# Gated linear attention and a normed MLP: the order of chunk 0, the rounding of the weights, and attention two chunks ahead

## The chip, the cores and the metric

One Trainium2 chip, one core of it. The metric is the device time of one execution in microseconds (us); the time before is 559.5 us, the median of three runs (559.44 to 559.54). The engines are named as in the profile: PE (TensorE, matrix products), DVE (VectorE), ACT (ScalarE), POOL (GpSimd) and SP (SyncE, which here only issues DMAs).

## The reference

Two blocks, one after the other. The first is a gated linear recurrence over 4 batches, 8 heads, 768 positions and heads of 48:

```
state = alpha[:, :, t, :, None] * state + k[:, :, t] (outer) v[:, :, t]
y[:, :, t] = q[:, :, t] @ state
```

Its output, reordered to (4, 768, 384), is `x` of the second block:

```
xn  = (x - mean) / sqrt(var + 1e-06) * g_ln
out = x + relu(xn @ w_ch1) @ w_ch2
```

`w_ch1` is 384 x 1536 and `w_ch2` 1536 x 384. Both arrive as 64-bit floats; everything else is 32-bit.

## The kernel before

**Chunks.** The 768 positions are cut into 6 chunks of 128 (`NCB`). Within a chunk the recurrence is done as matrix products, for each of the 4 batches apart, in five steps: `decays` (logarithm of alpha, running sum by a triangular matmul into `lps`, the exponentials `ek` and `eq`, `k*ek` on POOL and `q*eq` on DVE, the row of chunk gates sent through DRAM, the loads of the next chunk), `turn` (transposes into `tps`, copied to `qkT`), `scores` (`aps`, copied under a mask into `at`), `attend` (`yps`, the new state through `sps`, the copy to `x`, its mean and variance, the normed `xn`), and `turn_x` (transposes of `xn` into `xps`, multiplied by g into `xT`). `attention_steps(c)` lists these 20 steps as a wave: batch b is one step behind batch b - 1.

**The MLP.** For a chunk, all four batches together, `hidden(c, j)` makes one of the 12 blocks of 128 hidden units (3 contraction steps into `hps`, then a relu into `hT` on ACT for even j, on DVE for odd j). `project(c, b, js)` makes a third of the second product of one batch (`ops`), and with the last third adds `x` into `ob` and sends it out. In the profile a 32-bit product appears as two matmul instructions.

**Rounding.** The weights are loaded as 64-bit words in 12 pieces (6 of w1, then 6 of w2), each into one of three staging buffers (`STAGED`), and turned into 32-bit floats by seven DVE instructions a piece (`round_weights`, L129 to L138). `take_weights(i)` rounds piece i and then issues the load of piece i + 3 into the buffer that came free.

**Order.** `run(main, side)` lists the steps of `main` with those of `side` spread evenly between them. That list is the text's order; the framework's planner then orders each engine's instructions by priority of the text and by when its model has them ready, so that neighbours in the text may be mixed. Each engine works through its own list in order, and so does the queue of SP, in which a DMA that waits for a buffer holds up those behind it. Before the change the list is: attention of chunk 0 with w1's six roundings spread over it; the first product of chunk 0 with w2's six roundings and the first six steps of chunk 1's attention; then the second product of chunk 0 with the rest of them; and from then on, for each chunk, both products with the attention of the next chunk.

```
run(attention_steps(0), rounds[:half])
for c in range(NCB):
    side = attention_steps(c + 1) if c + 1 < NCB else []
    mlp = mlp_steps(c)
    if c == 0:
        run(mlp[:NJ], [go for i in range(half) for go in (rounds[half + i], side[i])])
        run(mlp[NJ:], side[half:])
    else:
        run(mlp, side)
```

PSUM has eight banks, shared out by tag: three for `lps`, `tps` and `aps`, two for `yps`, `sps` and `xps`, two for `hps`, one for `ops`.

Of the kernel before, what the change touches and what calls it, by code (L numbers as in the profile page):

```python
# [9 lines left out]
FP32 = mybir.dt.float32  # L10
# [4 lines left out]
AOP = mybir.AluOpType  # L15
# [6 lines left out]
def kernel(  # L22
# [8 lines left out]
    w_ch2: bass.AP,  # L31
    out: bass.AP,
):

# [14 lines left out]
    nc = tc.nc  # L51

    B, S, H, D = q.shape
    DM = H * D
    DF = w_ch1.shape[1]
    P = 128
    NCB = S // P
    NP = H // 2
    R = 64 + D
    NF = DM // P  # L60
    NJ = DF // P
# [3 lines left out]
    cpool = ctx.enter_context(tc.tile_pool(name="const", bufs=1))  # L65
    raw = ctx.enter_context(tc.tile_pool(name="raw", bufs=B))
    stage = ctx.enter_context(tc.tile_pool(name="stage", bufs=STAGED))
    work = ctx.enter_context(tc.tile_pool(name="work", bufs=2))
# [34 lines left out]
    pieces = []  # L103
    for i in range(NJ // 2):
        cs, js = slice(2 * i * P, 2 * (i + 1) * P), slice(2 * i, 2 * (i + 1))
        pieces.append((w1[:, :, cs], w1_src[:, :, cs]))
        pieces.append((w2[:, js], w2_src[:, js]))
    pieces = pieces[::2] + pieces[1::2]
    staged = {}

    def load_weights(i):
        if i >= len(pieces):
            return
        dst, src = pieces[i]
        if src.dtype != FP32:
            dst = staged[i] = stage.tile(list(dst.shape), INT64, name="ws", tag="ws")
        nc.sync.dma_start(dst, src)

    def round_weights(i):

        dst = pieces[i][0]
        ws = staged.pop(i)
        words = ws.bitcast(INT32).rearrange("p a (c t) -> p a c t", t=2)
        lo, hi = words[:, :, :, 0], words[:, :, :, 1]
        ts, stt = nc.vector.tensor_scalar, nc.vector.scalar_tensor_tensor
        ts(out=dst.bitcast(INT32), in0=hi, scalar1=0x000FFFFF, scalar2=0x00100000,  # L129
           op0=AOP.bitwise_and, op1=AOP.bitwise_or)  # L130
        stt(out=dst, in0=lo.bitcast(UINT32), scalar=2.0 ** -32, in1=dst.bitcast(INT32),  # L131
            op0=AOP.mult, op1=AOP.add)
        ts(out=lo, in0=hi, scalar1=0x7FF00000, scalar2=None, op0=AOP.bitwise_and)
        ts(out=lo, in0=lo, scalar1=float(896 << 20), scalar2=0.0,
           op0=AOP.subtract, op1=AOP.max)
        ts(out=hi, in0=hi, scalar1=-(1 << 31), scalar2=None, op0=AOP.bitwise_and)
        stt(out=hi, in0=lo, scalar=8.0, in1=hi, op0=AOP.mult, op1=AOP.add)  # L137
        stt(out=dst, in0=dst, scalar=2.0 ** -20, in1=hi.bitcast(FP32),  # L138
            op0=AOP.mult, op1=AOP.mult)

    def take_weights(i):
        if i in staged:
            round_weights(i)
        load_weights(i + STAGED)

    for i in range(STAGED):
# [1 line left out]

    eps = cpool.tile([P, 1], FP32, name="eps")
    nc.vector.memset(eps, EPS)  # L150


    eqs = [cpool.tile([P, NP, 2, 64], FP32, name=f"eq{b}") for b in range(B)]
# [38 lines left out]
    def turn(c, b):  # L192
        qkT = work.tile([R, 2, NP, P], FP32, name="qkT", tag="qkT", bufs=3)
        for i in range(2):
            tps = ps.tile([R, NP, P], FP32, name="tps", tag="a", bufs=3)
            for p in range(NP):
                nc.tensor.transpose(  # L197
                    tps[:, p], qks[b][:, i, p].rearrange("p a b -> p (a b)")[:, :R], ident)
            if i == 0:
                nc.scalar.copy(out=qkT[:, i], in_=tps)  # L200
            else:
                nc.vector.tensor_copy(out=qkT[:, i], in_=tps)  # L202
        qkT_of[c, b] = qkT
# [15 lines left out]
    def attend(c, b):  # L219
# [13 lines left out]
        if c + 1 < NCB:  # L233
# [6 lines left out]
            for i, s in heads:  # L240
# [1 line left out]
            st = sts[b].rearrange("p a b d -> p a (b d)")  # L242
            nc.gpsimd.tensor_mul(  # L243
                st, st, gate_of.pop((c, b)).unsqueeze(2).broadcast_to([P, NP, 2 * D]))
        x = work.tile([P, DM], FP32, name="x", tag="x", bufs=2 * B)
        nc.scalar.copy(out=x, in_=yps.rearrange("p a b d -> p (a b d)"))  # L246
        stats = work.tile([P, 6], FP32, name="stats", tag="stats")
        mv = work.tile([P, 2], FP32, name="mv", tag="mv")
# [10 lines left out]
    def turn_x(c, b):  # L259
        if b == 0:  # L260
            xT_of[c] = work.tile([P, NF, B, P], FP32, name="xT", tag="xT")
        xn = xn_of.pop((c, b))
        xps = ps.tile([P, NF, P], FP32, name="xps", tag="s")
        for f in range(NF):
            nc.tensor.transpose(xps[:, f], xn[:, f * P:(f + 1) * P], ident)  # L265
        nc.vector.tensor_mul(xT_of[c][:, :, b], xps,  # L266
                             g_col.unsqueeze(2).broadcast_to([P, NF, P]))

    def hidden(c, j):
        if j == 0:
            hT_of[c] = work.tile([P, NJ, B, P], FP32, name="hT", tag="hT", bufs=1)
        hps = ps.tile([P, B, P], FP32, name="hps", tag="h")
        for f in range(NF):
            nc.tensor.matmul(hps, w1[:, f, j * P:(j + 1) * P], xT_of[c][:, f],  # L276
                             start=(f == 0), stop=(f == NF - 1))
        if j % 2 == 0:
            nc.scalar.activation(out=hT_of[c][:, j], in_=hps, func=AFT.Relu)  # L279
        else:  # L280
            nc.vector.tensor_scalar_max(hT_of[c][:, j], in0=hps, scalar1=0.0)  # L281

    ops_of = {}

    def project(c, b, js):
        if js[0] == 0:
            ops_of[b] = ps.tile([P, DM], FP32, name="ops", tag="o", bufs=1)
        for j in js:
            nc.tensor.matmul(ops_of[b], hT_of[c][:, j, b], w2[:, j],  # L289
                             start=(j == 0), stop=(j == NJ - 1))  # L290
        if js[-1] == NJ - 1:
            ob = work.tile([P, DM], FP32, name="ob", tag="ob", bufs=3)
            nc.vector.tensor_add(ob, ops_of.pop(b), x_of.pop((c, b)))  # L293
            nc.sync.dma_start(out[b, c * P:(c + 1) * P], ob)

    def attention_steps(c):

        stages = [decays, turn, scores, attend, turn_x]
        return [lambda f=stages[w - b], b=b: f(c, b)
                for w in range(B + len(stages) - 1)  # L300
                for b in range(B) if 0 <= w - b < len(stages)]

    def mlp_steps(c):
        thirds = [range(i * NJ // 3, (i + 1) * NJ // 3) for i in range(3)]
        return ([lambda j=j: hidden(c, j) for j in range(NJ)]
                + [lambda b=b, js=js: project(c, b, js) for b in range(B) for js in thirds])

    def run(main, side):

        done = 0  # L310
        for i, step in enumerate(main):
            step()
            due = (i + 1) * len(side) // len(main)
            for go in side[done:due]:
                go()
            done = due

    half = len(pieces) // 2
    rounds = [lambda i=i: take_weights(i) for i in range(len(pieces))]
    run(attention_steps(0), rounds[:half])  # L320
    for c in range(NCB):
        side = attention_steps(c + 1) if c + 1 < NCB else []
        mlp = mlp_steps(c)
        if c == 0:
            run(mlp[:NJ], [go for i in range(half) for go in (rounds[half + i], side[i])])
            run(mlp[NJ:], side[half:])
        else:
            run(mlp, side)


# [27 lines left out]
```

## Time and profile before

| | before |
|---|---|
| median of three runs | 559.5 us |
| the profiled execution's own time | 557.12 us |
| its span | 555.3 us |
| PE busy | 519.0 us (93%) |
| DVE busy | 225.0 us (41%) |
| ACT busy | 90.1 us (16%) |
| POOL busy | 50.4 us (9%) |
| granted clock of PE, mean | 0.966 |
| share of PE in the chain that ended last | 88%, of DVE 7%, of DMA 3% |

The table is from the page of the profiled execution. Busy time is what an engine spent on instructions; matmuls are pipelined, so their busy times overlap and a PE that is busy all the time is not one at its peak. The clock is the share of TensorE's full speed that was granted.

### The profile page before, as it was taken

The page shows a single profiled execution, that of the slowest core. Times are in us where ns is not written, and L with a number is a line of the kernel's source. Part 1 is how long each engine was busy: PE and PEld are TensorE (multiplying, and loading weights), DVE is VectorE, ACT ScalarE, POOL GpSimd, SP SyncE. Part 2 cuts the span into 40 slices and gives each one's busy share as a digit, 9 for nine tenths or more (in the row PEclk, how much of TensorE's full clock was granted, in tenths as well). Part 3 has the DMA queues.
Part 4 walks back from the last instruction along what each step waited for, and adds up shares of the span by engine and source line. Part 5 has one row for each costly group of instructions (what it writes and reads, how often), then busy time and mean ns, then how long its engine had stood idle before and what let it go on. Part 6 is the DMA issues. An engine that isn't in the chain of part 4 may idle for free.

```text
span 555.3 us, 7418 instructions
## 1 busy us (share of the span) xinstructions
PE 519.0 (93%) x3112; PEld 303.0 (55%) x3112; DVE 225.0 (41%) x385; ACT 90.1 (16%) x205; POOL 50.4 (9%) x54
## 2 busy tenths in 40 slices
PE   4665699999899999999999999999999999999997
PEld 2454244666545566645566644666645566644553
DVE  2999999533422432423432423331433322311000
ACT  3211021111212210122200032200122110101000
POOL 3232000110200100100100010010101000000000
PEclk9856699999999999999999999999999999999999
DMA  8975343220121110122120011110000000000000
GB/s 271 301 215 191 96 146 99 59 86 30 56 60 44 43 43 30 44 54 63 28 71 30 30 57 45 29 43 15 15 15 0 1 14 15 16 14 1 4 24 28
DMA packets 32489, 33.72 MB, mean 61 GB/s; under 512 B 13108, under 2 KB 28596, under 8 KB 32456
## 3 DMA queue, kind: packets, MB, share of 16 engines
q1 hardware_dynamic: 31912, 33.12, 19.5%
q8 instruction: 24, 0.39, 0.3%
q10 hardware_dynamic: 544, 0.13, 0.1%
q14 instruction: 9, 0.07, 0.0%
HBM read 28.49 MB, written 4.76 MB: 60 GB/s over the span
## 4 chain that ended last, share of the span: by engine, by line
PE 88%; DVE 7%; DMA 3%; issue 1%; POOL 0%; SPq 0%; POOLq 0%; DVEq 0%
PE ops L289 35%; PE hps L276 34%; PE aps L212 4%; PE yps L231 4%; PE yps L226 3%; PE tps L197 3%; PE lps L176 2%; PE sps L238 1%; PE xps L265 1%; DMA ws<-in_moe_w_ch_dram 1%; DVE ws L137 1%; DVE w L131 1%; DVE w L129 1%; DVE w L138 1%; DMA ra<-in_alpha_dram 1%
## 5 line engine op out<-in xcount | busy, mean ns | idle before, releaser
L289 PE MATMUL ops<-w,hT 128*128 128x384 f32 x576 | 198.3, 492 | 2.0 <-DVE ob L293 2.0
L276 PE MATMUL hps<-xT,w 128*128 128x512 f32 x432 | 195.8, 601 | 1.8 <-DVE xT L266 1.8
L289 PEld LDWEIGHTS ops<-w,hT 128*128 128x128 f32 x576 | 105.5, 190 | 69.7 <-DVE ob L293 3.8
L276 PEld LDWEIGHTS hps<-xT,w 128*128 128x128 f32 x432 | 80.3, 192 | 93.4 <-issue 84.8
L281 DVE TENSOR_SCALAR hT<-hps 128x512 f32<-128x512 f32 x36 | 24.8, 690 | 83.7 <-PE hps L276 83.4
L181 POOL TENSOR_TENSOR qk<-rk,ek 128x384 f32<-128x384 f32 x24 | 28.5, 1187 | 212.6 <-ACT ek L179 205.2
L279 ACT ACTIVATE hT<-hps 128x512 f32<-128x512 f32 x36 | 21.5, 597 | 117.9 <-PE hps L276 117.9
L215 DVE COPY_PREDICATED at<-consts,aps 128x512 f32<-128x512 int32 x48 | 32.5, 719 | 18.9 <-PE aps L212 18.8
L231 PE MATMUL yps<-rv,at 128*64 128x48 f32 x768 | 39.8, 230 | 0.0
L231 PEld LDWEIGHTS yps<-rv,at 128*64 128x64 f32 x768 | 35.5, 149 | 3.9 <-issue 3.9
L241 DVE TENSOR_TENSOR st<-sps,st 64x192 f32<-64x192 f32 (+1 forms) x40 | 14.2, 355 | 57.0 <-PE sps L238 56.7
L293 DVE TENSOR_TENSOR ob<-ops,x 128x384 f32<-128x384 f32 x24 | 13.4, 558 | 55.8 <-PE ops L289 55.4
L246 ACT COPY x<-yps 128x384 f32<-128x384 f32 x24 | 11.5, 478 | 150.4 <-PE yps L231 150.3
L243 POOL TENSOR_TENSOR st<-st,gate 128x384 f32<-128x384 f32 x20 | 18.6, 928 | 182.4 <-DVE st L241 151.4
L197 PE MATMUL tps<-consts,qk 128*112 128x128 f32 x192 | 27.8, 286 | 7.2 <-DVE qk L182 5.4
L197 PEld LDWEIGHTS tps<-consts,qk 128*112 128x112 f32 x192 | 22.9, 139 | 19.4 <-issue 9.7
L182 DVE TENSOR_TENSOR qk<-rq,eq 128x384 f32<-128x384 f32 x24 | 23.3, 969 | 25.1 <-ACT eq L180 25.1
L212 PEld LDWEIGHTS aps<-qkT 48*128 48x128 f32 x384 | 25.7, 204 | 13.7 <-issue 9.0
L212 PE MATMUL aps<-qkT 48*128 48x128 f32 x384 | 30.7, 303 | 0.0
L176 PE MATMUL lps<-la,consts 128*128 128x384 f32 x48 | 22.1, 544 | 8.2 <-ACT la L174 4.3
L226 PE MATMUL yps<-st,qkT 112*64 112x96 f32 x320 | 29.7, 259 | 0.0
L202 DVE COPY qkT<-tps 112x512 f32<-112x512 f32 x24 | 16.5, 689 | 31.3 <-PE tps L197 31.3
(33 smaller groups left out, 252.9 us busy)
## 6 DMA issues: line engine op xcount, KB each, us to landing
ws<-in_moe_w_ch_dram SPq DMA_DIRECT2D x12, 768.0 KB, 4.7
ra<-in_alpha_dram SPq DMA_DIRECT2D x24, 192.0 KB, 3.0
rk<-in_k_dram SPq DMA_DIRECT2D x24, 192.0 KB, 3.4
rq<-in_q_dram SPq DMA_DIRECT2D x24, 192.0 KB, 2.5
rv<-in_v_dram SPq DMA_DIRECT2D x24, 192.0 KB, 2.4
out_dram<-ob SPq DMA_DIRECT2D x24, 192.0 KB, 1.8
row<-eq SPq DMA_DIRECT2D x20, 2.0 KB
gate<-row SPq DMA_DIRECT2D x20, 2.0 KB, 2.9
```

The lines of the kernel that those rows point to most:

```text
L176: nc.tensor.matmul(lps[:, :DM], tri, la, start=True, stop=True)
L181: nc.gpsimd.tensor_mul(qk[:, 1, :, :D], raws.pop(("k", c, b)), ek)
L182: nc.vector.tensor_mul(qk[:, 0, :, :D], raws.pop(("q", c, b)), eq)
L197: nc.tensor.transpose(tps[:, p], qks[b][:, i, p].rearrange("p a b -> p (a b)")[:, :R], ident)
L212: nc.tensor.matmul(aps[i][:, p], qkT[rows, 1, p], qkT[rows, 0, p], start=True, stop=True)
L215: nc.vector.copy_predicated(out=at[:, i], data=aps[i], mask=mask.unsqueeze(1).broadcast_to([P, NP, P]))
L226: nc.tensor.matmul(yps[s, p].rearrange("p a b -> p (a b)"), qkT[:, 0, p, s], sts[b][:R, p].rearrange("p a b -> p (a b)"), start=True, stop ...
L231: nc.tensor.matmul(yps[s, p, i], at[:, i, p, s], vt[:, 2 * p + i], start=(c == 0), stop=(c == 0 or i == 1))
L276: nc.tensor.matmul(hps, w1[:, f, j * P:(j + 1) * P], xT_of[c][:, f], start=(f == 0), stop=(f == NF - 1))
L279: nc.scalar.activation(out=hT_of[c][:, j], in_=hps, func=AFT.Relu)
L281: nc.vector.tensor_scalar_max(hT_of[c][:, j], in0=hps, scalar1=0.0)
L289: nc.tensor.matmul(ops_of[b], hT_of[c][:, j, b], w2[:, j], start=(j == 0), stop=(j == NJ - 1))
```

## The change

The attention of chunk 0 is listed alone. Then come w1's roundings, each followed by two blocks of the first product of chunk 0, with the attention of chunk 1 spread over them; then w2's six roundings in a row. After that each chunk's list is its second product and the next chunk's first product, with the attention of the chunk after next. The second product goes through batches in pairs, third by third. `hps` and `ops` share one PSUM tag with three buffers. The gain g is multiplied into w1's rows in the last rounding instruction, which becomes three; `xT` becomes a plain copy on ACT. In chunk 0 all relus are on ACT, and in chunk 1 both copies of `qkT` are. `x` has 12 buffers in place of 8.

```diff
-    pieces.append((w1[:, :, cs], w1_src[:, :, cs]))
-    pieces.append((w2[:, js], w2_src[:, js]))
+    pieces.append((w1[:, :, cs], w1_src[:, :, cs], True))
+    pieces.append((w2[:, js], w2_src[:, js], False))
...
-        stt(out=dst, in0=dst, scalar=2.0 ** -20, in1=hi.bitcast(FP32),
-            op0=AOP.mult, op1=AOP.mult)
+        if not gains:
+            stt(out=dst, in0=dst, scalar=2.0 ** -20, in1=hi.bitcast(FP32),
+                op0=AOP.mult, op1=AOP.mult)
+            return
+        for f in range(NF):
+            stt(out=dst[:, f], in0=dst[:, f], scalar=g20[:, f:f + 1],
+                in1=hi[:, f].bitcast(FP32), op0=AOP.mult, op1=AOP.mult)
...
+    g20 = cpool.tile([P, NF], FP32, name="g20")
+    nc.gpsimd.tensor_scalar_mul(g20, g_col, 2.0 ** -20)
...
-            if i == 0:
+            if i == 0 or c == 1:
                 nc.scalar.copy(out=qkT[:, i], in_=tps)
...
-        x = work.tile([P, DM], FP32, name="x", tag="x", bufs=2 * B)
+        x = work.tile([P, DM], FP32, name="x", tag="x", bufs=3 * B)
...
-        nc.vector.tensor_mul(xT_of[c][:, :, b], xps,
-                             g_col.unsqueeze(2).broadcast_to([P, NF, P]))
+        nc.scalar.copy(out=xT_of[c][:, :, b], in_=xps)
...
-        hps = ps.tile([P, B, P], FP32, name="hps", tag="h")
+        hps = ps.tile([P, B, P], FP32, name="hps", tag="m", bufs=3)
...
-        if j % 2 == 0:
+        if c == 0 or j % 2 == 0:
             nc.scalar.activation(out=hT_of[c][:, j], in_=hps, func=AFT.Relu)
...
-            ops_of[b] = ps.tile([P, DM], FP32, name="ops", tag="o", bufs=1)
+            ops_of[b] = ps.tile([P, DM], FP32, name="ops", tag="m", bufs=3)
...
-    def mlp_steps(c):
+    def hidden_steps(c):
+        return [lambda j=j: hidden(c, j) for j in range(NJ)] if c < NCB else []
+
+    def project_steps(c):
+
         thirds = [range(i * NJ // 3, (i + 1) * NJ // 3) for i in range(3)]
-        return ([lambda j=j: hidden(c, j) for j in range(NJ)]
-                + [lambda b=b, js=js: project(c, b, js) for b in range(B) for js in thirds])
+        return [lambda b=b, js=js: project(c, b, js)
+                for b0 in range(0, B, 2) for js in thirds for b in range(b0, min(b0 + 2, B))]
...
-    run(attention_steps(0), rounds[:half])
+    for step in attention_steps(0):
+        step()
+    first = hidden_steps(0)
+    run([go for i in range(half) for go in (rounds[i], *first[2 * i:2 * i + 2])],
+        attention_steps(1))
+    for go in rounds[half:]:
+        go()
     for c in range(NCB):
-        side = attention_steps(c + 1) if c + 1 < NCB else []
-        mlp = mlp_steps(c)
-        if c == 0:
-            run(mlp[:NJ], [go for i in range(half) for go in (rounds[half + i], side[i])])
-            run(mlp[NJ:], side[half:])
-        else:
-            run(mlp, side)
+        side = attention_steps(c + 2) if c + 2 < NCB else []
+        run(project_steps(c) + hidden_steps(c + 1), side)
```

## Rows read from the trace of the kernel before

**Rows 1.** Table of stages: busy us (x instructions) by engine, granted clock, DMA share.

```profile
core 0: us, PE busy (x) PEld busy (x) DVE busy (x) ACT busy (x) POOL busy (x), PEclk, DMA share, GB/s
0.00:61.50 61.50, 33.26 (x310) 24.71 (x310) 49.99 (x88) 14.88 (x34) 17.85 (x19) 0.73 0.72 224
61.50:98.70 37.20, 37.20 (x108) 17.86 (x109) 36.41 (x57) 6.04 (x11) 1.00 (x1) 0.95 0.37 123
...
147.50:151.30 3.80, 2.30 (x14) 1.63 (x15) 2.81 (x6) 1.91 (x6) 2.09 (x2) 1.00 0.32 94
...
234.40:319.20 84.80, 84.79 (x540) 49.55 (x540) 28.67 (x50) 14.73 (x34) 7.31 (x8) 1.00 0.17 48
```

**Rows 2.** Chain of waits, head and last chunk: start, us, what.

```profile
59.13 0.39 DVE xn L255
59.52 0.87 DVE w L131
...
61.51 12.46 PE hps L276 x24
...
487.03 31.17 PE hps L276 x72
...
526.58 8.02 PE ops L289 x24
```

**Rows 3.** Waits of PE: who waits for whom, us in total, times, longest.

```profile
PE xps L265 <- DVE xn L255: 13.6, 3, 6.5
...
PE ops L289 <- DVE ob L293: 2.0, 3, 0.7
```

**Rows 4.** Timeline, chunk 0's first batches and one of chunk 1: start, us, what.

```profile
4.31 1.65 PE L176 MATMUL lps<-la,consts 128*128 128x384 f32 x2 [4.31 <-ACT la L174]
...
16.27 0.91 PE L176 MATMUL lps<-la,consts 128*128 128x384 f32 x2
...
18.28 0.48 ACT L246 COPY x<-yps 128x384 f32<-128x384 f32 x1
...
103.26 0.48 ACT L246 COPY x<-yps 128x384 f32<-128x384 f32 x1 [2.99 <-PE yps L231]
...
105.93 0.48 DVE L255 TENSOR_SCALAR xn<-x,mv,rstd 128x384 f32<-128x384 f32 x1 [0.60 <-ACT rstd L253]
```

**Rows 5.** Timeline of DVE: rounding instructions of w1 (first) and w2.

```profile
16.04 0.95 DVE L129 TENSOR_SCALAR w<-ws 128x768 int32<-128x768 int32 x1
...
83.98 0.55 DVE L129 TENSOR_SCALAR w<-ws 128x768 int32<-128x768 int32 x1
...
84.92 0.55 DVE L136 TENSOR_SCALAR ws<-ws 128x768 int32<-128x768 int32 x1
85.39 0.95 DVE L131 SCALAR_TENSOR_TENSOR w<-ws,w 128x768 f32<-128x768 uint32 x1
86.25 0.95 DVE L137 SCALAR_TENSOR_TENSOR ws<-ws 128x768 int32<-128x768 int32 x1
```

**Rows 6.** Groups by line and form: count, busy us, mean ns, idle before.

```profile
L281 DVE TENSOR_SCALAR hT<-hps 128x512 f32<-128x512 f32 x36 | 24.8, 690 | 83.7 <-PE hps L276 83.4
...
L279 ACT ACTIVATE hT<-hps 128x512 f32<-128x512 f32 x36 | 21.5, 597 | 117.9 <-PE hps L276 117.9
...
L202 DVE COPY qkT<-tps 112x512 f32<-112x512 f32 x24 | 16.5, 689 | 31.3 <-PE tps L197 31.3
...
L266 DVE TENSOR_TENSOR xT<-xps,g_col 128x384 f32<-128x384 f32 x24 | 13.3, 555 | 26.4 <-PE xps L265 26.4
```

**Rows 7.** Timeline of POOL: three multiplications by `ek`.

```profile
17.84 2.41 POOL L181 TENSOR_TENSOR qk<-rk,ek 128x384 f32<-128x384 f32 x1 [3.58 <-ACT ek L179]
...
27.91 3.68 POOL L181 TENSOR_TENSOR qk<-rk,ek 128x384 f32<-128x384 f32 x1 [3.37 <-DVE ws L133]
...
81.30 1.00 POOL L181 TENSOR_TENSOR qk<-rk,ek 128x384 f32<-128x384 f32 x1 [25.71 <-ACT ek L179]
```

**Rows 8.** Timeline of the SP queue: two loads of pieces.

```profile
59.16 7.63 SPq L117 DMA_DIRECT2D ws<-in_moe_w_ch_dram  x2
```

More of the change, by code (lines that the diff above doesn't have):

```diff
@@ L113, in load_weights @@
             return
-        dst, src = pieces[i]
+        dst, src, _ = pieces[i]
         if src.dtype != FP32:
@@ L119, in round_weights @@
     def round_weights(i):
-        dst = pieces[i][0]
+        dst, _, gains = pieces[i]
         ws = staged.pop(i)
@@ L143, in take_weights @@
             round_weights(i)
+        elif pieces[i][2]:
+            for f in range(NF):
+                nc.vector.tensor_scalar_mul(pieces[i][0][:, f], pieces[i][0][:, f],
+                                            g_col[:, f:f + 1])
         load_weights(i + STAGED)
```

## The prediction

> **What bounds the kernel now.** I read the table of stages first. TensorE is full (37.2 of 37.2 us, 84.8 of 84.8) from 61.5 us on, at granted clock 0.95 to 1.00; before that it is busy 33.3 of 61.5 us at a mean clock of 0.73, with DVE busy 50.0 [rows 1]. So there are two regimes: a head that DVE sets, and a body that TensorE sets. The chain of waits says the same: up to 61.51 us it hops between rounding instructions and norms of chunk 0 on DVE, and the first product (`hps`, L276) begins there; from there it is almost only TensorE [rows 2]. TensorE's longest waits are 13.6 us for `xn` of chunk 0, and 2.0 us, in three waits, for the output addition `ob` [rows 3]. Body work that only changes places is worth nothing. What counts is when the body begins, what idle time enters it, and what the few idles in it come to.
>
> The body's unit prices, at full clock: one chunk's first product 31.2 us (72 matmuls), its second about 8.0 us a batch with the norm's wait left out, 32 us in all [rows 2]. A whole period is 84.8 us [rows 1], so one chunk of attention costs TensorE about 22 us.
>
> **The change part by part.** I call T1 the moment of the first `hps` matmul. It is 61.5 us before.
>
> *Attention of chunk 0 without rounding in its text order.* TensorE, ACT, POOL and the SP loads of chunk 0 stay the same instructions; only DVE's rounding is moved behind them. Batches 0 and 2 send their first matmul (`lps`) at 4.31 and 16.27 us [rows 4], while rounding had hardly begun (its first instruction stands at 16.04 [rows 5]). So a batch follows every 6.0 us, and batch 3 would begin at 22.3. Batch 0 takes from 4.31 to the end of its `x` copy at 18.76 [rows 4], 14.5 us. From such an end to the end of `xn`, with DVE free, it is 106.41 - 103.74 = 2.7 us [rows 4]; then a transpose and a copy, about 1 us (estimate: the multiplication that writes `xT` now takes 0.56 [rows 6]). So a batch takes 18.2 us, and batch 3 is through at 40.5. Part of batch 0 ran at the lower clock: its `lps` took 1.65 us against 0.91 for batch 2's [rows 4]. Four such steps of TensorE, each about 0.8 us shorter, give 3.3 back: T1 = 37 us. Bounds: 33, if the engines follow each other closer than batches 0 to 2 did; 57, if rounding fills DVE in front of the norms as it does now.
>
> *w1's rounding piece by piece, with the first product and chunk 1's attention.* On DVE in dense stretches, short rounding instructions stand 0.47 us apart and long ones 0.86 (84.92, 85.39, 86.25 [rows 5]). A piece of w2 is four short and three long, 4.5 us; of w1, whose first instruction is long too (0.95 against 0.55 [rows 5]), 4.9. The last instruction is now three, each over a third of the columns. No row shows that form: between 0.86 for all three (nothing but columns counts) and 3 x 0.47; I take 1.0, near the first since the columns are the same, so 5.0 us a piece, 30 us for six. w2's six cost 27. Chunk 1's attention: DVE is busy 28.7 us in a full period [rows 1], of which six evictions of `hps` at 0.69, four copies of `qkT` at 0.69 and four of `xT` at 0.56 [rows 6] go to ACT in this stage: 19.6 us, in which four output additions stand that this stage lacks and overlaps that a dense stretch saves; I take 15. So a third of a chunk's rounding pair (one piece, two `hps` steps, 3.3 attention steps) costs DVE 5.0 + 2.5 = 7.5 us and TensorE 5.2 + 3.7 = 8.9. TensorE is the longer: this stage takes it 31.2 + 22 = 53 us, from 37 to 90, and DVE's rounding hides beside it. ACT gains 12 evictions in place of 6 (0.60 each [rows 6]) and a few copies, some 8 us in over 50, where it was busy 6 of 37 [rows 1]: nothing.
>
> *w2's rounding as a block of six.* If DVE goes on as it does from 61.5 to 98.7 (36.4 of 37.2 us busy [rows 1]), it has after T1 five pieces of w1 (25), attention (15) and w2 (27): done at 37 + 67 = 104. The second product of batches 0 and 1 now runs in thirds side by side, two pieces for each pair of thirds: 5.3 us of products and 2 us of chunk 2's attention. It wants piece 2 of w2 at 90 (there at 86), piece 4 at 97 (at 95), piece 6 at 105 (at 104). It just fits. For what does not, S = 4 us of TensorE idle, between 0 and the 13 of the second rival.
>
> *DMA queues.* SP's loads of w1's pieces 4 to 6 and all of w2 wait in SP's queue for a staging buffer, as two did before (7.63 us [rows 8]); behind them stand chunk 1's gate rows and chunk 2's loads. The gates are wanted by chunk 2's attention and the loads likewise, at 90 us or later. Three buffers at 7.5 us a piece leave 15 us for a load. Nothing.
>
> *g folded into w1* makes `xT`'s multiplication a copy on ACT: 0.56 us off DVE, about as much on ACT, neither on the body's path. One small POOL instruction in the prologue is hidden under loads.
>
> *Three PSUM buffers shared by both products.* The three waits for `ob` go: -2.0 us [rows 3]. The last addition and the transfer behind it stay.
>
> *Attention two chunks ahead.* The gap at 147.5 to 151.3, where TensorE is busy 2.3 of 3.8 us [rows 1], comes from chunk 2's attention being wanted just as it ends. With a chunk of slack this kind of wait should shrink; I take -1 us of 1.5, bounds 0 and -1.5. The four further buffers of `x` add no instruction.
>
> **A rule that speaks against it.** Two of POOL's multiplications of chunk 0 took 2.41 and 3.68 us while DVE rounded, and one that met a quieter DVE 1.00 [rows 7]. The new order puts rounding beside chunk 1's eight POOL instructions too. The Trainium skill (SBUF — State Buffer, "Who interferes with whom") says that GpSimd and VectorE share a pair of ports as an exclusive lock, so that the one that comes second is shut out until the other has finished; these rows agree. By it all eight could be late by up to 2.7 us; that is the third rival, worked out below from the rows alone.
>
> **The sum**, against the profiled execution's own span: T1 37 + what followed T1 before, 555.3 - 61.5 = 493.8, - 2.0 - 1.0 + S 4 = 531.8 us. The profiled execution's own time is 557.1, 1.8 above its span, and the median of the runs 559.5 is 4.2 above that span; the same 4.2 gives 536 us.
>
> **Rivals.**
> 1. *The fill stretches the head.* DVE's order in the trace mixes rounding and attention more finely than the text (L131 of one piece stands right behind `xn` on the chain [rows 2]). If all six pieces of w1 are pulled ahead among chunk 0's norms, T1 stays near 57 and the rest is TensorE's: 57 + 493.8 - 3 = 547.8, so 552 us. For it: free slots on DVE exist while TensorE transposes. Against: the trace's rounding began where the text has it, after the first scores, and three buffers allow three pieces; half of it (T1 45, S 3) gives 543.
> 2. *w2 starves the second product.* If DVE keeps the text's order strictly, w2's block begins only when chunk 1's attention is done, at 90, and lasts to 117; TensorE has 10.6 us of thirds and some 4 of attention for those 27: idle 13 in place of 4, so 545 us. For it: nothing of w2 comes earlier in the text. Against: rounding depends on a load alone, and dense DVE stretches exist in rows 1.
> 3. *POOL is shut out.* Eight instructions, each 2.7 us late and each on TensorE's path: 21 us in place of 4, 553 us. Against: the third row shows one that was not late beside rounding, and products stand between the steps.
> 4. *Slower: DVE and TensorE take turns.* Where an attention step on DVE waits for a matmul that is queued behind products, and the next rounding waits behind that step, each piece costs 5.0 + 8.9 instead of the longer: 6 x 13.9 = 83 us instead of 53, then 13 of rival 2. That is 30 + 13 = 43 in place of 4: 575 us. It decides against the change from the point where idle in the new stage passes the 24.5 us that T1 gains plus 3. Against: from 61.5 to 98.7 both engines were full at once with the same kind of mixture [rows 1].
> 5. *Nothing gained* (the planner restores the old order, T1 61.5): 555.3 - 3, 557 us.
>
> **How the numbers follow.** Forecast 0.58 (T1 33 to 41, S 0 to 6: 527 to 542); rival 1 0.14, rival 2 0.15, rival 3 0.04, rival 4 0.05, rival 5 0.01, and 0.03 for still better (T1 under 33). Predicted 536. The range, 526 to 549, holds the forecast, rival 2 and the milder half of rival 1. A measurement of this kernel tells about 0.2% (1.1 us) from no change. Faster: everything but rival 4 and a part of rivals 3 and 5: 0.93; within 0.2%: 0.01; slower: 0.06.
>
> **What would show it.** In the table of stages, the first `hps` at 33 to 41 us; TensorE over 90% busy from there to 105; no waits for `ob` at the end; rounding of w2 over by about 104. Rival 1 shows as a first `hps` past 45, rival 2 as TensorE waiting for the last rounding line just ahead of `ops` (L289's place), rival 3 as waits of `tps` for POOL, rival 4 as idle TensorE at every piece. The forecast is wrong if the period of 84.8 us itself changes, which no part of the sum allows for.

## The result, and the profile after

The changed kernel takes 534.46 us (median of 4 runs, 533.18 to 537.34); the kernel before, timed on the same chip, takes 559.47 (558.61 to 559.54). The ratio is 0.9563, with an interval of 0.9523 to 0.9604. Forecast were 536 us and a range of 526 to 549. The profiled execution took 534.97 us, with a span of 533.3.

The two regimes are still there, and they meet earlier. The table of stages of the kernel after, to set beside [rows 1]:

```profile
core 0: us, PE busy (x) PEld busy (x) DVE busy (x) ACT busy (x) POOL busy (x), PEclk, DMA share, GB/s
0.00:44.90 44.90, 29.39 (x342) 21.91 (x343) 34.00 (x65) 18.74 (x43) 15.73 (x21) 0.97 0.80 245
44.90:100.10 55.20, 52.11 (x409) 29.41 (x407) 52.26 (x92) 17.04 (x37) 9.57 (x5) 0.93 0.54 166
100.10:125.00 24.90, 23.99 (x102) 14.57 (x100) 16.78 (x26) 4.92 (x12) 3.16 (x3) 1.00 0.27 72
186.30:270.50 84.20, 84.18 (x542) 49.52 (x541) 26.50 (x47) 16.78 (x38) 7.31 (x8) 1.00 0.17 48
```

The reader is to see three things. The head has lost a third of its DVE work (50.0 us busy before, 34.0 now) and TensorE nearly half of its idle time there (28.2 us idle before, 15.5 now). The new stage from 44.9 to 100.1, which carries first product, rounding and chunk 1's attention at once, keeps TensorE busy 94% and DVE 95%. And a period of the steady body is 84.2 us, not 84.8.

The waits of TensorE, over the whole span (who waits for whom, us in total, times, longest), beside [rows 3]:

```profile
PE xps L279 <- DVE xn L269: 6.2, 4, 2.9
PE tps L211 <- DVE at L229: 4.8, 3, 3.1
PE lps L190 <- ACT la L188: 4.4, 1, 4.4
PE tps L211 <- DVE qk L196: 3.9, 2, 3.5
PE tps L211 <- PE aps L226: 0.2, 1, 0.2
```

The 13.6 us for `xn` are 6.2, and no wait for `ob` is left. The end of the chain of waits (start, us, what) shows what the second of these brings: the last chunk's second product is one unbroken piece, where before it was four of 8 us with an addition between [rows 2].

```profile
498.79 30.97 PE ops L302 x96
529.76 0.02 issue
529.79 0.56 DVE ob L306
```

Cut at the first `hps` (T1) and at the last chunk's second product, the two profiled executions differ so. The cuts of before are 61.51, 518.19 and 551.92 us, those of after 44.92, 498.79 and 529.76.

| stretch | before | after | difference | forecast |
|---|---|---|---|---|
| start to T1 | 61.5 | 44.9 | -16.6 | -24.5 |
| T1 to the last second product | 456.7 | 453.9 | -2.8 | +3.0 |
| last second product | 33.7 | 31.0 | -2.8 | -2.0 |
| what follows it | 3.4 | 3.5 | +0.2 | 0 |
| span | 555.3 | 533.3 | -22.0 | -23.5 |

So the total was met within 2 us by a head that gained 7.9 us less than forecast and a rest that gained 6.4 more. The experiments take both apart. T1 of after, in the timeline of TensorE (start, us, engine, line; in brackets the idle time ahead and its releaser):

```profile
22.54 0.81 PE L190 MATMUL lps<-la,consts 128*128 128x384 f32 x2
42.67 0.90 PE L279 MATMUL xps<-consts,xn 128*128 128x128 f32 x3 [2.89 <-DVE xn L269]
44.92 9.82 PE L289 MATMUL hps<-xT,w 128*128 128x512 f32 x18
82.14 0.62 PE L211 MATMUL tps<-consts,qk 128*112 128x128 f32 x4 [3.09 <-DVE at L229]
```

Batch 3 of chunk 0 begins where it was forecast (22.54 us; 22.3 worked out). It ends late, and the timeline of DVE in front of that `xn` gives a part of the reason: four rounding instructions of w1 (L132, L134, L136) stand between the end of `x` at 36.94 and `xn`.

```profile
35.94 1.80 DVE L132 TENSOR_SCALAR w<-ws 128x768 int32<-128x768 int32 x2
37.66 0.94 DVE L134 SCALAR_TENSOR_TENSOR w<-ws,w 128x768 f32<-128x768 uint32 x1
38.53 0.71 DVE L255 TENSOR_TENSOR st<-sps,st 64x192 f32<-64x192 f32 x2
39.27 0.56 DVE L263 BATCH_NORM_STATS2 stats<-x 128x6 f32<-128x384 f32 x1
39.75 0.81 DVE L136 TENSOR_SCALAR ws<-ws 128x768 int32<-128x768 int32 x1
40.48 0.17 DVE L264 BATCH_NORM_AGGREGATE mv<-stats 128x2 f32<-128x6 f32 x1
40.58 1.65 DVE L134 SCALAR_TENSOR_TENSOR w<-ws,w 128x768 f32<-128x768 uint32 x1
42.15 0.47 DVE L269 TENSOR_SCALAR xn<-x,mv,rstd 128x384 f32<-128x384 f32 x1
```

The last of the four took 1.65 us, the same instruction at 37.66 only 0.94. Beside it ran a multiplication on POOL, in the timeline of POOL:

```profile
40.11 1.31 POOL L195 TENSOR_TENSOR qk<-rk,ek 128x384 f32<-128x384 f32 x1
```

### The profile page after: what moved, and what is told of

Its sections match the earlier page's. It is cut to its first block, busy times and chain, and to the rows that moved or that the text cites. A ratio compares the mean times of both kernels' runs of the same rounds, so it can differ in the third digit from the quotient of the medians.

```text
span 533.3 us, 7434 instructions
## 1 busy us (share of the span) xinstructions
PE 510.2 (96%) x3112; PEld 297.9 (56%) x3112; DVE 209.0 (39%) x363; ACT 106.8 (20%) x239; POOL 52.4 (10%) x55
## 4 chain that ended last, share of the span: by engine, by line
PE 83%; DVE 11%; DMA 2%; issue 2%; SPq 1%; ACT 0%; DVEq 0%; ACTq 0%
PE ops L302 34%; PE hps L289 33%; PE aps L226 3%; PE tps L211 3%; PE yps L240 3%; PE yps L245 3%; PE lps L190 2%; PE xps L279 1%; DMA ws<-in_moe_w_ch_dram 1%; PE sps L252 1%; DVE w L134 1%; DVE at L229 1%; DVE w L132 1%; DVE st L255 1%; DVE w L146 1%
## 5 line engine op out<-in xcount | busy, mean ns | idle before, releaser
L289 PE MATMUL hps<-xT,w 128*128 128x512 f32 x432 | 199.8, 607 | 0.0
L302 PE MATMUL ops<-w,hT 128*128 128x384 f32 x576 | 194.2, 488 | 0.0
L302 PEld LDWEIGHTS ops<-w,hT 128*128 128x128 f32 x576 | 107.0, 190 | 69.8 <-issue 0.5
L292 ACT ACTIVATE hT<-hps 128x512 f32<-128x512 f32 x42 | 25.1, 597 | 128.3 <-PE hps L289 128.3
L294 DVE TENSOR_SCALAR hT<-hps 128x512 f32<-128x512 f32 x30 | 20.8, 692 | 73.0 <-PE hps L289 72.6
L195 POOL TENSOR_TENSOR qk<-rk,ek 128x384 f32<-128x384 f32 x24 | 31.2, 1298 | 183.0 <-ACT ek L193 183.0
L229 DVE COPY_PREDICATED at<-consts,aps 128x512 f32<-128x512 int32 x48 | 32.4, 722 | 13.9 <-PE aps L226 13.6
L245 PE MATMUL yps<-rv,at 128*64 128x48 f32 x768 | 36.6, 219 | 0.0
L245 PEld LDWEIGHTS yps<-rv,at 128*64 128x64 f32 x768 | 32.3, 138 | 1.2 <-issue 1.1
L214 ACT COPY qkT<-tps 112x512 f32<-112x512 f32 x28 | 16.1, 584 | 56.0 <-PE tps L211 56.0
L193 ACT ACTIVATE ek<-lps 128x384 f32<-128x384 f32 x24 | 11.8, 490 | 69.7 <-PE lps L190 69.5
```

The source lines that it names most:

```text
L195: nc.gpsimd.tensor_mul(qk[:, 1, :, :D], raws.pop(("k", c, b)), ek)
L229: nc.vector.copy_predicated(out=at[:, i], data=aps[i], mask=mask.unsqueeze(1).broadcast_to([P, NP, P]))
L245: nc.tensor.matmul(yps[s, p, i], at[:, i, p, s], vt[:, 2 * p + i], start=(c == 0), stop=(c == 0 or i == 1))
L302: nc.tensor.matmul(ops_of[b], hT_of[c][:, j, b], w2[:, j], start=(j == 0), stop=(j == NJ - 1))
```

## The experiments

Theory: the order of the steps carries the gain, by an earlier T1; what is missing of the forecast T1 was lost to w1's rounding, which still stands ahead of chunk 0's norms on DVE. Rivals: the side edits (`g`, PSUM, output order) carry it; or the head is set by its own chain and rounding costs nothing there. Every run is compared with runs of the kernel before on the same chip.

**old_order.** The old list of steps, with all the rest of the change.

```diff
-    for step in attention_steps(0):
-        step()
...
+    run(attention_steps(0), rounds[:half])
+    for c in range(NCB):
+        side = attention_steps(c + 1) if c + 1 < NCB else []
+        mlp = hidden_steps(c) + project_steps(c)
+        ...
```

> The new kernel with the old list of steps alone (rounding spread over chunk 0's attention, w2's rounding beside the first product, attention one chunk ahead); g folded, copies on ACT, shared PSUM tag and pairs stay. Theory: the gain is the earlier first product (44.9 us against 61.5). With the old order it begins at 57 to 61, and the time is 553 us (549 to 556): 559.5 less 2.0 for the output additions' waits and some 3 to 5 for instructions that left DVE. Rival, that the side edits carry the gain: 540 us or less.

Measured: 553.62 us, ratio 0.9913 (0.9894 to 0.9933). The first `hps` is back where it was, in the timeline of TensorE:

```profile
62.39 13.16 PE L289 MATMUL hps<-xT,w 128*128 128x512 f32 x24 [0.57 <-ACT xT L280]
```

So the side edits alone gain 4.7 us and the order the other 19 or so. The side edits' part is seen in this trace: the last second product is again one piece of 30.97 us (-2.8), and a period is 84.4 us instead of 84.8. The list holds two changes, an early T1 and attention two chunks ahead; `one_ahead` below takes the second away.

**light_w1.** The rounding of w1 without all but its first instruction, so that w1 holds no weights.

```diff
         ts(out=dst.bitcast(INT32), in0=hi, scalar1=0x000FFFFF, scalar2=0x00100000, ...)
+        if gains:
+            return
```

> The new kernel, in which a piece of w1 is rounded by its first instruction only (the other eight are left out, so w1 holds no weights). Theory: rounding instructions in front of chunk 0's norms on DVE made the first product begin at 44.9 us and not at the 37 that was forecast. Then it begins at 37 to 40, the 4 us of idle behind it shrink to 1 or 2, and the time is 526 us (522 to 529). Rival, that the chain of engines itself needs until 43 or later: the first product begins at 43 to 45 and the time is 531 us or more.

Measured: 529.94 us, ratio 0.9487 (0.9470 to 0.9504). T1, in the timeline of TensorE:

```profile
41.43 7.94 PE L291 MATMUL hps<-xT,w 128*128 128x512 f32 x18
```

This lies between the two expectations: T1 is 3.5 us earlier, and the total 4.5 us. `x` of batch 3 ends at 36.69 us here and at 36.94 in the kernel after; `xn` ends at 40.20 here and at 42.62 there. The timeline of DVE in this run:

```profile
39.04 1.16 DVE L271 TENSOR_SCALAR xn<-x,mv,rstd 128x384 f32<-128x384 f32 x1 [0.83 <-ACT rstd L269]
```

So 2.2 of the 3.5 us lie between `x` and `xn`, where the four rounding instructions stood, and 1.1 between `xn` and the first `hps`, where the kernel after runs at half clock. Both halves of the theory hold in part: rounding in the head costs some of T1, and the chain of chunk 0, with the first instructions of the pieces still beside it, needs 41.4. The size is uncertain, since each T1 is from one profiled execution: the change profiled again (`after_again`) has its T1 at 43.60, 1.3 us earlier. The 18 matmuls behind T1 take 7.94 us here and 9.82 in the kernel after: 1.9 us more, which is the clock (below).

**unpaired.** The second product batch by batch, in place of two batches side by side in thirds.

```diff
-                for b0 in range(0, B, 2) for js in thirds for b in range(b0, min(b0 + 2, B))]
+                for b in range(B) for js in thirds]
```

> The new kernel with the second product batch by batch in place of in pairs. Theory: w2's last piece is ready at 112 us, and batch 0's last third is now wanted near 107, so TensorE waits about 5 us once: 539 us (537 to 541). Rival, that chunk 2's attention fills the wait or that pairs matter elsewhere: within 1 us of the new kernel (534.5), or a loss spread over all chunks.

Measured: 535.46 us, ratio 0.9576 (0.9554 to 0.9597), no different from the change by its interval. My theory fell: in the trace no wait of TensorE names w2, and between 100 and 125 us TensorE is idle for 1.5 us against 0.9 in the change. Steps of chunk 2's attention stand where the wait was expected, so the pairs cover little that isn't covered already.

**old_psum.** `unpaired`, and the two products with the PSUM buffers of before (two for `hps`, one for `ops`).

```diff
-        hps = ps.tile([P, B, P], FP32, name="hps", tag="m", bufs=3)
+        hps = ps.tile([P, B, P], FP32, name="hps", tag="h")
...
-            ops_of[b] = ps.tile([P, DM], FP32, name="ops", tag="m", bufs=3)
+            ops_of[b] = ps.tile([P, DM], FP32, name="ops", tag="o", bufs=1)
```

> The new kernel with the second product batch by batch and the old PSUM tags (two buffers for hps, one for ops). Against the run that differs in the batches alone (535.5 us) the theory wants the three waits for the output addition back, 2.0 us, all in the last chunk: 537.5 us (537 to 538.5). Rival, that with attention two chunks ahead other chunks' seams are bare too: 3 us or more above 535.5, with more than three such waits.

Measured: 540.19 us, ratio 0.9672 (0.9636 to 0.9708), 4.7 above `unpaired`. Its profiled execution has a span 3.0 us longer than that of `unpaired`, and the chain of waits has 2.8 of them in the last second product, which is again in four:

```profile
499.61 7.75 PE ops L302 x24
507.36 0.02 issue
507.39 0.57 DVE ob L306
507.96 0.04 issue
508.00 8.02 PE ops L302 x24
...
525.32 8.02 PE ops L302 x24
533.34 0.03 issue
```

From 499.61 to 533.34 are 33.73 us, as in the kernel before (518.19 to 551.92), against 30.97 in one piece. Each break costs the wait (0.64) and 0.27 us more of the matmuls behind it (8.02 against 7.75), so 2.8 and not the 2.0 of the row of waits alone. The median lies beyond the expected 537 to 538.5 and in the range of the rival, but the rival's reason isn't seen: the waits for `ob` come to 2.1 us, and all but 0.2 of it is in the last chunk. Why the median differs by 4.7 is not settled.

**one_ahead.** w1's and w2's rounding as in the change, but attention only one chunk ahead, beside the second product alone.

```diff
...
+    for c in range(NCB):
+        side = attention_steps(c + 1) if c + 1 < NCB else []
+        run(project_steps(c), side)
+        for go in hidden_steps(c + 1):
+            go()
```

> The new kernel with attention one chunk ahead: chunk 0's attention, w1's rounding with the first product and nothing beside it, w2's rounding, then each second product with the next chunk's attention, and the next first product alone. Theory: chunk 1's attention is what fills TensorE while DVE rounds; without it TensorE has 31 us of products for 52 us of rounding, and later chunks end on the last norm with nothing beside it, as before the change: 540 us (536 to 545). Rival, that the planner pulls chunk 1's attention up by itself and the slack of a chunk is worth nothing: within 1.5 us of 534.5.

Measured: 544.72 us, ratio 0.9743 (0.9712 to 0.9775). TensorE waits at the seam of every chunk (its waits, as above):

```profile
PE tps L211 <- DVE qk L196: 11.3, 7, 3.3
PE xps L279 <- DVE xn L269: 9.6, 4, 4.3
```

These are 7.4 and 3.4 us more than in the change. Its T1 is 41.67, 3 us before that of the change, and it ends 10 us later. Attention two chunks ahead and its spread over both products, which this run takes away together, are worth those 10 us in this order of the head. So T1 alone doesn't carry the gain of the order: from `old_order` to this run, with T1 some 21 us earlier, are 9 us, and from this run to the change another 10.

**late_loads.** The loads of w1's pieces 2 and 3 held back until the last norm of chunk 0, so that they can't be rounded earlier. A small copy of `rstd` into the buffer makes the load wait.

```diff
-        nc.sync.dma_start(dst, src)
+            if late:
+                nc.scalar.copy(out=dst.bitcast(FP32)[:, 0, :1], in_=after)
+        (nc.scalar if late else nc.sync).dma_start(dst, src)
...
-    for i in range(STAGED):
-        load_weights(i)
+    load_weights(0)
...
+        if (c, b) == (0, B - 1):
+            for i in range(1, STAGED):
+                load_weights(i, rstd)
```

> The new kernel; the loads of w1's pieces 2 and 3 go through ACT's queue and wait (by a one-column copy into the staging buffer) for the norm of chunk 0's last batch, so that only piece 1 can be rounded ahead of it. Nothing is left out. Theory, that rounding in front of the last norms costs 3.5 us of T1 (44.9 against the 41.4 of the run with w1's rounding cut): the first product begins at 41 to 42.5; piece 2 lands near 46, is rounded by 51, about when it is wanted, so idle behind T1 grows by 0 to 3 us: 532.5 us (530 to 535). Rival, that the early pieces were needed and rounding now runs behind: TensorE waits at w1's pieces and w2's, 537 us or more.

Measured: 541.60 us, ratio 0.9692 (0.9666 to 0.9718). The theory that early rounding is pure loss fell; the rival held. The chain got little shorter (the last `xT` copy ends at 43.6 us, at 44.1 in the change), and TensorE runs chunk 1's attention from there until the first product begins at 50.62. Of the pieces loaded late, one has its first rounding instruction at 46.55, but the next in DVE's list is the first of another piece, which lands at 52.2 with DVE idle. The first product then waits for this rounding, as the timelines of DVE and of TensorE show:

```profile
52.21 0.95 DVE L135 TENSOR_SCALAR w<-ws 128x768 int32<-128x768 int32 x1 [4.71 <-DMA ws<-in_moe_w_ch_dram]
```

```profile
50.62 5.42 PE L294 MATMUL hps<-xT,w 128*128 128x512 f32 x12
...
59.82 3.66 PE L294 MATMUL hps<-xT,w 128*128 128x512 f32 x5 [2.77 <-DVE w L149]
```

So the pieces taken in the head are worth more than they cost there, against pieces that come this late. The run held back loads and rounding together, and DVE waits 1.7 and 4.7 us for the loads themselves. What early rounding alone is worth, with the loads in place, was not tested.

**bits** and **late_bits.** The rounding in three instructions of shifts and masks (the low bits are cut off), `g` by three short multiplications; `late_bits` holds the loads back as well.

```diff
...
+        bits = dst.bitcast(INT32)
+        ts(out=bits, in0=hi, scalar1=3, scalar2=0x3FFFFFFF,
+           op0=AOP.logical_shift_left, op1=AOP.bitwise_and)
+        stt(out=bits, in0=lo, scalar=29, in1=bits,
+            op0=AOP.logical_shift_right, op1=AOP.bitwise_or)
+        stt(out=bits, in0=hi, scalar=-(1 << 30), in1=bits,
+            op0=AOP.bitwise_and, op1=AOP.bitwise_or)
+        if gains:
+            for f in range(NF):
+                ts(out=dst[:, f], in0=dst[:, f], scalar1=g_col[:, f:f + 1], scalar2=None,
+                   op0=AOP.mult)
```

> The new kernel with another rounding: the 32-bit pattern is put together by shifts and masks in three DVE instructions (low bits cut off, not rounded), and g multiplied in by three short ones for w1. By the trace's spacings a piece of w2 costs 2.2 us of DVE in place of 4.5, of w1 3.2 in place of 5.0: some 25 us less of DVE in the head. Theory, that DVE sets the head: the first product begins at 39 to 42, idle behind it under 2 us, 528 us (524 to 531). Rival, that the chain of chunk 0's attention sets it: 532 us or more.

> The same late loads with the three-instruction rounding by shifts and masks (low bits cut off). The run with that rounding alone began the first product at 49.2 us, later than the new kernel, with less DVE work: by the theory because its short pieces were put in front of the norms, not because of their cost. With the loads held back the first product begins at 40 to 42 and rounding then needs only 3.2 us a piece: 529 us (526 to 532). Rival, that the 49.2 comes from elsewhere (the lower granted clock while it waits): the first product begins at 45 or later, 533 us or more.

Measured: `bits` 534.53 us, ratio 0.9549 (0.9503 to 0.9594); `late_bits` 535.52, 0.9578 (0.9550 to 0.9606). Some 40% of the rounding work gone (its lines keep DVE busy 40.4 us in `bits`, 68.9 in the change), and nothing gained in the median. `bits` begins the first product at 49.23, later than either expectation had it. Cheaper rounding was pulled further ahead: two of its instructions stand in front of `at` of batch 2 on DVE, though its scores were done at 27.9 us. TensorE then waits 3.19 us for `xn`, and its next matmuls run at half clock (32 `yps` in 1.95 us; after a wait of 1.38 us they took 1.20 in the kernel after). The timeline of DVE:

```profile
27.84 0.94 DVE L133 TENSOR_SCALAR w<-ws 128x768 int32<-128x768 int32 x1
...
29.93 1.27 DVE L135 SCALAR_TENSOR_TENSOR w<-ws,w 128x768 int32<-128x768 int32 x1
...
31.31 1.32 DVE L224 COPY_PREDICATED at<-consts,aps 128x512 f32<-128x512 int32 x2
```

The timeline of TensorE behind it:

```profile
33.06 0.90 PE L274 MATMUL xps<-consts,xn 128*128 128x128 f32 x3 [3.19 <-DVE xn L264]
33.89 1.95 PE L240 MATMUL yps<-rv,at 128*64 128x48 f32 x32
...
49.23 10.46 PE L284 MATMUL hps<-xT,w 128*128 128x512 f32 x24
```

One run of `bits` had a mean granted clock of 0.997 and took 529.58 us; in the profiled one, with 0.987, it took 535.38. This made a second theory: what remains in the head is the granted clock. In `late_bits` the first product begins at 44.35 and waits 3.58 us for a piece further on, as in `late_loads`.

**after_again.** The change once more, in five rounds, to see how its own times go with the clock.

> The new kernel again, beside the two below on one chip. All theories: 534.5 us (533 to 537.5), and the faster of its runs have the higher mean granted clock.

Measured: 535.09 us (533.10 to 535.48), ratio 0.9575 (0.9556 to 0.9594). No clean order: 533.10 at 0.993, but 535.13 at 0.994. By the mean clock alone the spread of this kernel is not explained. The profiled execution, of the same kernel, has this T1 in place of 44.92 (timeline of TensorE):

```profile
43.60 9.18 PE L289 MATMUL hps<-xT,w 128*128 128x512 f32 x18
```

**bits_act.** `bits` with the multiplication by `g` on ACT.

```diff
-                ts(out=dst[:, f], in0=dst[:, f], scalar1=g_col[:, f:f + 1], scalar2=None,
-                   op0=AOP.mult)
+                nc.scalar.mul(dst[:, f], dst[:, f], g_col[:, f:f + 1])
```

> The rounding by shifts and masks with g multiplied in on ACT, so that DVE has three instructions a piece and no short ones. Theory A (DVE's amount of rounding in the head costs up to 4.5 us, as the run with w1's rounding cut showed): the first product begins at 42 to 45, 531 us (529 to 533). Theory B (what counts is which instructions the planner puts in front of chunk 0's scores and norms, not their amount): no better than the run with three short DVE multiplications, 533 to 536 us, first product at 46 or later.

Measured: 530.29 us (528.83 to 532.94), ratio 0.9508 (0.9484 to 0.9532). T1 is 45.44, no earlier than after, but at full clock (18 `hps` in 7.89 us); two runs at 0.989 and 0.990 took 532.94 and 532.39, the four at 0.993 to 0.997 took 528.83 to 530.34. The time is where theory A had it and T1 between the two, so this run doesn't decide between them.

**bits_hi2** and **warm.** `bits_hi2` takes the rounding to two instructions (high words only) and puts chunk 0's `qkT` copies on ACT: the least DVE work of all. `warm` is `bits_hi2` with twelve matmuls that nobody reads, behind the transposes and the scores of batches 1 to 3 of chunk 0.

```diff
+            if c == 0 and b > 0 and f in (turn, scores):
+                for i in range(2):
+                    junk = ps.tile([P, 2 * P], FP32, name="junk", tag="m", bufs=3)
+                    ...
+                    nc.tensor.matmul(junk, m[:, :P], m, start=True, stop=True)
```

> Two DVE instructions a piece: the high words alone are shifted and masked (the low 3 of 23 mantissa bits stay zero), g is multiplied in on ACT, and chunk 0's copies of qkT are on ACT too. Its list on DVE has all six instructions of three pieces ahead of chunk 0's third scores and none between there and the last norm. Theory A: 529.5 us (527 to 531), first product at 40 to 42, TensorE idle behind it under 3 us. Theory B gives the same here, since nothing stands in front of the last norms; a first product later than 44 speaks against both and for the clock or ACT.

> The run with two rounding instructions a piece (532.5 us), with 12 matmuls more in chunk 0 whose result nobody reads: two of 256 columns each behind the transposes and the scores of batches 1 to 3, where TensorE waited in short gaps. At full clock they take 0.43 us each, 5.2 us in all. In the run without them TensorE ran at granted clock 0.5 from 24 to 41 us, which doubled some 8 us of matmuls. Theory (gaps of TensorE in front of 24 us made the clock fall, and the fall cost T1): the clock from 20 to 40 us is 0.9 or more, the first product begins at 42 to 45 in place of 47.8, 527.5 us (524 to 530). Rival (the clock falls regardless, or the additional matmuls delay the chain by as much as they save): 532 us or more.

Measured: `bits_hi2` 532.48 us, ratio 0.9533 (0.9514 to 0.9552); `warm` 528.56 us (527.27 to 531.99), ratio 0.9472 (0.9444 to 0.9500). T1 of `bits_hi2`, in the timeline of TensorE:

```profile
47.84 9.64 PE L281 MATMUL hps<-xT,w 128*128 128x512 f32 x18
```

Both theories had it at 40 to 42, so neither the amount of DVE's rounding nor what stands in front of the last norms sets this head by itself. Its table of stages, from 20 to 40 us:

```profile
20.00:40.00 20.00, 17.68 (x153) 13.77 (x154) 12.36 (x25) 9.56 (x25) 3.48 (x4) 0.60 0.62 181
```

The same stretch of `warm`:

```profile
20.00:40.00 20.00, 17.94 (x237) 14.40 (x235) 14.86 (x29) 12.29 (x31) 4.48 (x5) 1.00 0.72 205
```

With DVE busy only 12.4 of 20 us, `bits_hi2` ran its head at 0.60 of full speed; TensorE is busy 17.68 us there and gets through 153 matmul instructions; in the change it was 15.42 us for 231. With the twelve matmuls it is 1.00. That gains 3.9 us, and the intervals of the two ratios lie apart. T1 (the timeline of TensorE in `warm`) isn't where I had it:

```profile
47.07 10.57 PE L281 MATMUL hps<-xT,w 128*128 128x512 f32 x24
```

I had expected 42 to 45. The added matmuls stand in the chain themselves, and some more of chunk 1's attention is done by T1. The two profiled spans, 531.8 and 526.7 us, differ by 5.1. Of these T1 is 0.8, and about 1.8 are the 18 matmuls behind it, which `bits_hi2` ran at half clock for the most part (9.64 us; 7.89 in `bits_act`). A wait of 1.4 us for `at` at 82 us, which `warm` doesn't have there, is not the clock; the rest is not traced. So the clock carries a part of the gain, not shown to be all. `warm` has the lowest median of all that ran, below both kernels; since it leaves the low words out of the weights, its rounding is not that of the change.

## Why the prediction was right, and where it wasn't

*The two regimes* held: what moved the time was when the body begins and what idle time enters it, and the order alone carries about 19 of the 24 us (`old_order`). T1 is not the whole of it: `one_ahead`, with T1 at 41.67, keeps about half of the 19, and the rest hangs on attention two chunks ahead and its spread over both products, for which the sum has 1 us.

*T1 = 37 us* was wrong: 44.9, outside the 33 to 41 of the forecast, though inside the wide bounds of 33 to 57. Its terms, one by one. The start of batch 3: 22.3 forecast, 22.54 measured. From its `lps` to the end of `x`: 14.5 forecast, 14.4 measured, at a granted clock of 1.00. So the 3.3 us that I gave back for full clock were the first mis-sized term (four times the 0.74 between its two rows would have been 3.0): the clock was full and the discount gave nothing. It wasn't the rounding that ate it: in `light_w1`, also at full clock, that `x` ends at 36.69, where the sum without the discount has 36.8. That the steps of the other engines set the length of a batch is likely, but not shown. From `x` to the end of `xn`: 2.7 forecast "with DVE free", 5.7 measured, since DVE was not free; that is the second. In `light_w1` it is 3.5, so rounding costs 2.2 of the 5.7, and 0.8 was missing from the 2.7 even without it (`xn` itself took 1.16 us there, 0.47 in the change). From there to the first `hps`: 1.0 forecast, 2.3 measured, at half clock; 1.2 in `light_w1`, at full clock. Without the discount the working gives 40.5, and `light_w1`, with most of the rounding gone, has 41.4.

*The first rival* is therefore half true: T1 is at its "half of it (T1 45)". Its price of 543 was as wrong as my T1, because T1 alone is not the body's position. TensorE had used its head for about 3 us of chunk 1's attention before T1 (an estimate from the 32 instructions more, 342 against 310 of the kernel before), and nothing in my sum credits that.

*S = 4 us*: the waits of TensorE behind T1 are 3.1, 0.6 and 0.4 us, 4.0 in all. But they aren't where I put them. The largest is `tps` for `at` at 82.14, not w2 ahead of the second product: the scores were done at 77.6 us, and four rounding instructions stand in front of that `at` on DVE, as they did in front of `xn`. w2's rounding ended at 112.1, where I had 104; that is 67.2 us behind T1, and 67 were forecast. The first `ops` came at 100.2, where I had 90, so it just fitted as worked out, only later. The lower clock behind T1 and around 82 costs about 3.6 us (estimate from the clock of each 2 us), where the kernel before lost 2.2 behind its own T1: a term that I left out.

*The `ob` waits*: -2.0 forecast, -2.8 measured; the break in the product costs a little beside the wait (`old_psum`).

*The gap at 147.5*: -1 forecast; it is gone, as is one of 0.8 us at 487, together -2.3.

*The period*, of which I wrote that no part of the sum allows for a change: 84.8 to 84.2 us in the steady ones, of which each trace has two; over five periods that would be -3 us, an estimate. `old_order` has 84.4, `old_psum` 84.3, `unpaired` 84.2, so neither the order nor the PSUM buffers carry it alone. Its cause isn't settled.

For the middle these make -3.1 + 4.0 + 1.4 - 2.3 - 3.0 = -3.0, and the measured difference is -2.8. The forecast total was met because a T1 that was 7.9 us too early and gains that I had left out nearly cancel, and that is luck in part.

*Rivals 2, 4 and 5* didn't happen: no wait of TensorE names w2's rounding, there is no idle time per piece, and T1 moved. *Rival 3*, POOL shut out, didn't happen as priced. One multiplication by `ek` took 6.08 us beside dense rounding, more than any in [rows 7]:

```profile
69.31 6.08 POOL L195 TENSOR_TENSOR qk<-rk,ek 128x384 f32<-128x384 f32 x1 [6.27 <-ACT ek L193]
```

No wait of TensorE names POOL here, since products stand between the steps, as the prediction said against it. The row agrees with the exclusive lock that the Trainium skill (SBUF — State Buffer, "Who interferes with whom") describes. But the price can fall on DVE as well, and the prediction missed that in its own third row. It calls DVE quieter there, and DVE was as dense; POOL had begun first, and it was DVE that took longer, in its timeline in the kernel before:

```profile
81.68 1.44 DVE L138 SCALAR_TENSOR_TENSOR w<-w,ws 128x768 f32<-128x768 f32 x1
```

The same instruction takes 0.95 us in dense stretches. So it was in the head of the change: L134 at 40.58, on the path to T1, took 0.7 us more beside POOL.

*The price of w1's last instruction* as three short ones: 1.0 us estimated; in dense stretches they stand 0.40 us apart, 1.2 to 1.3 in all. It decided nothing.

## What to carry to other kernels

When a long job moves out of the way of a latency-bound chain on an in-order engine, work out the chain with that job's instructions standing in front of each of its links, not with the engine free. Don't drive the job out of the head altogether either: here, with loads and rounding both held back, the next stage waited for it. Read the body's gain from work done, not from the moment at which one landmark instruction starts. A head in which TensorE waits in short pieces can pay in clock too. In one version here twelve matmuls that nobody reads brought the clock back and gained more than they cost, though they stood in the chain.

## What was unexpected of the hardware

With less work the head was slower: `bits_hi2` has the lightest DVE load of the versions without added matmuls, and its TensorE ran at a granted clock of 0.60 from 20 to 40 us, 0.50 (the level of 1.2 GHz) for most of it, where the kernel after, with the heavier rounding, ran at 1.00 up to 40 us. What brought the clock down is open: in front of 24 us TensorE waited 0.39, 0.77 and 0.83 us in `bits_hi2`, and the clock fell, and 0.61 and 1.95 us in `light_w1`, and it stayed at 1.00. In the kernel after, the clock column is 1.00 until TensorE has been idle for 2.89 us in front of `xps` at 42.67; then it is 0.50 until 48, and back at full speed soon after. (The column says 1.00 from the start, but `lps` took 1.65 us at 4.38 and 0.91 at 16.57, so it doesn't give the speed of the first matmuls.) By 2 us:

```profile
40.00:42.00 2.00, 0.00 (x0) 0.00 (x0) 2.00 (x3) 0.50 (x2) 1.42 (x2) 0.99 0.65 186
42.00:44.00 2.00, 1.32 (x5) 0.79 (x5) 2.00 (x5) 0.39 (x1) 0.00 (x0) 0.50 0.38 98
...
46.00:48.00 2.00, 2.00 (x3) 0.78 (x3) 2.00 (x6) 0.00 (x0) 0.00 (x0) 0.50 0.40 118
48.00:50.00 2.00, 2.00 (x5) 0.86 (x4) 2.00 (x4) 0.37 (x1) 0.00 (x0) 0.80 0.69 140
```

In `light_w1` TensorE waits 0.95 us in front of the same `xps`, and the 18 matmuls behind it take 7.94 us instead of 9.82. So this fall costs 1.9 us in these matmuls, on top of the wait itself.
